# One core, state-space block and maxout FFN: full-array unread products, chunk 2's masks on GpSimd, a new order of the steps, weight-sum parts on VectorE

## Chip, cores and metric

One core of a Trainium2 chip. Times are device microseconds of one execution. The kernel before takes 240.26 us (median of 3 runs, 239.38 to 270.97). The profiled execution has its own time, 239.82 us, and a span of 238.1 us from its first to its last instruction.

## The reference, cut to what matters

Two blocks follow each other. The first is a chunked state-space scan for 4 batches, 8 heads, 768 positions, head dimension 32 and state size 16. Within a chunk:

```
cum = cumsum(log(clip(a)));  L = exp(cum_i - cum_j), causal
y  = ((C B^T) * L) x  +  (C state) * exp(cum)
state = exp(sum) * state + sum_j exp(cum_end - cum_j) B_j x_j
```

The result, 3072 tokens by 256 features, goes through a maxout FFN:

```
h   = max(max(y @ w1, y @ w2), y @ w3)      # w: 256 x 768
out = h @ w_out                             # 768 x 256
```

The weights come in as 64-bit floats and everything else as 32-bit.

## The kernel before

The sequence is cut into six chunks c = 0..5 of 128 positions, each of two halves g of 64. Feature groups of the FFN are f = 0..5, 128 wide; the weights are loaded and decoded in groups f0 = 0 (one f wide), 1 (one), 2 (two) and 4 (two).

What each engine does is a list of small named steps. The string ORDER at the top holds some 1,090 step names, and the program issues them in that order; `name/v` puts a step on another engine than its own (a ScalarE, v VectorE, p GpSimd, s SyncE's DMA queue, t TensorE). Every engine works its own steps strictly in this order, and a step waits for the tiles that it reads and for the buffer that it takes over. So the order is written out by hand in ORDER, and buffers of a kind (SLOTS; `ps` are the eight PSUM banks) are handed on in the order in which they come free.

Steps that the text speaks of:

- `ident`, `mask`, `ones`, `esel` and others (lines 200 to 282) make constants. `d.if0` loads group f0 of weight i (0, 1, 2 are w1, w2, w3; `o` is w_out), 64 bits as pairs of words, `ab cl sh lo pl sg` decode them to 32 bits (lines 640 to 675; `pl` on GpSimd), `df` subtracts w2 from w1 or w3 (`dd`), and `h.`/`l.` split a tile into a rounded high and a low part (`parts`, lines 677 to 684), since every product is made of three: high times high, high times low, low times high.
- `a.* clip ln scan pt0 pd1 pt1 left` make the running sum of log a for three spans of positions (0 to 128, 128 to 256, the rest), as bf16 parts in `left`. `right.c.p` copies rows of it by DMA on SyncE's queue. `mm.c.b` puts a mask into a PSUM bank by a product with a 128 x 128 identity (`mask_mm`, line 337), `em` (or `e` where no mask is there) adds the differences of the sums (`e_mm`), `xp` is the exponential on ScalarE into `L`. Where no mask product was made, `sel.c.p.g` sets the upper triangle to zero on GpSimd (`select`, line 365), four of them a chunk. Chunks 0, 1 and 2 use `mm`, chunks 3, 4 and 5 `sel`.
- `lB lC tB tC` load and transpose B and C of chunks 1 to 5 in 32 KB pieces; chunk 0 uses `lt`, `ltC` with turns on TensorE (`trB`, `trC`). `En E` are the decays from the chunk's start, `cd` or `ce` C times them, `bd` or `bk` B with its decay (`Bd`), `s` the scores C B (line 506), `w` the scores times `L` on VectorE, `A S so sa` the state, `yo` the product with the old state (line 518), `yw` the product within the chunk (line 530; `yw.c.g` for one half). `yH yL` split y.
- `up.c.f.i` (line 799) makes y @ (w1 - w2) or y @ (w3 - w2) for chunks 0, 1: six 512-column products, or a half with a fourth number; `m h hH hL` make the maximum and its parts.
- Chunks 2, 3 and 4, 5 go in pairs: seven products in place of eight per f (`q1` to `q7`, three matmuls each, line 818), for which differences `T.c.j` of the y parts and sums `ss` of the weight differences are made. `sw.f0.j` makes the four parts of `ss`, `h.ss`/`l.ss` split them. For groups 2 and 4 such a tile is 128 x 1024. `x1 e2 g7 c1 c2 mx hb ha hR hM` combine the seven.
- w2 itself, which the differences leave out of the maximum, is folded into w_out (`bt`, `b`, `fold`, `fo`), and `dn.c.term.z` (line 892) adds six h terms and two y terms, three parts each, into the output banks; `ob` copies them out, `st` stores them.
- `warm.n` (line 963) is a 512-column product of `ones`, whose result nobody reads. Eight stand at the very end of ORDER.

Of the kernel before, what the change touches and what calls it, by code (L numbers as in the profile page):

```python
# [29 lines left out]
xp.1.3 E.1 xp.1.2 lB.1.3 sh.02 left.2 s.0 mm.1.1 em.1.0 En.3 w.0.0 lx.0 En.2 mm.2.2 xp.1.1  # L30
w.0.3 xp.1.0 w.0.1 d.04 df.22 E.2 A.0 mm.2.1 w.0.2 yw.0.0 S.0.0 lB.1.5 E.3 lB.1.7 lB.1.0 ab.04
yH.0.0.0 pl.02 sg.02 df.02/v cl.04 sh.04 mm.2.3 yH.0.1.0 lB.1.6 h.up22 lB.1.2 lo.04 l.up22
pl.04 lB.1.1 tB.1 yo.0 yw.0.1 yH.0.1.1 yH.0.0.1 yL.0.0.0 h.up02 d.14 lo.14 tk.1 right.2.1
right.2.2 lC.1.3 yL.0.1.0 yL.0.1.1 ab.14 yL.0.0.1 En.5 right.2.0 em.2.1 S.0.1 d.24 ab.24 E.5
up.0.2.1 lC.1.7 lC.1.0 l.up02/v lC.1.5 up.0.3.0 so.0.1/v xp.2.2 xp.2.3 cl.14 sg.04 lC.1.4
sh.14 bk.1 m.0.3 lC.1.2 lC.1.1 lC.1.6 tC.1 lx.1 up.0.2.0 pl.14 sg.14 cd.1 df.04/v cm.1.1 cl.24
up.0.3.1 h.0.3 cm.1.0 s.1 m.0.2 h.0.2 sa.0.1 h.up04 l.up04/v w.1.3 mm.2.0 d.10 A.1 d.20 em.2.0
lo.24 right.3.0 up.0.5.0 xp.2.0 S.1.0 d.00 so.1.0 sh.24 lB.2.1 lB.2.4 w.1.1 sa.1.0 pl.24
xp.2.1 w.1.2 yo.1 w.1.0 ab.00 cl.00 lo.20 d.11 lC.2.4 lB.3.6 m.0.5 bt.2 ab.11 lC.3.4 sg.24
yw.1 cl.11 lC.3.7 df.24/v lo.10 ab.20 cl.20 lo.00/v lo.11/v h.up24 l.up24/v ab.10 cl.10  # L40
yH.1.1.0 lC.3.1 lB.4.4 h.b4 d.o2 sh.00 ab.o2 sh.10 sh.20 pl.10 yH.1.1.1 pl.00 right.3.1
yH.1.0.1 l.b4 hH.0.2 lB.2.2 up.0.4.0 up.0.5.1 S.1.1 yH.1.0.0 pl.20 lC.2.0 d.21 right.3.2
lB.2.3 up.0.4.1 yL.1.1.1 m.0.4 yL.1.1.0 yL.1.0.0 d.01 e.3.1 yL.1.0.1 xp.3.3 lo.01 sg.20 ab.01
sg.00 sg.10 up.1.4.0 df.00 h.0.5 up.1.2.0 sw.2.2 lC.2.1 lC.2.3 cl.01 sh.11 h.up00/v lC.4.1
lB.2.5 lB.3.5 up.1.4.1 lB.3.1 lC.3.5 pl.11 hH.0.3 df.20/v right.4.0 sh.01 lB.2.6 m.1.2 ab.21
sg.11 bt.1 h.up20/v bt.0 l.up20 lB.2.7 lo.21 lC.2.5 up.1.5.1 h.b2 m.1.4/v xp.3.2 h.1.4 pl.01
sg.01 d.o4 cl.21 lo.o2 l.up00/v h.b0 sw.4.2 sh.21 cl.o2 l.b0 lB.2.0 ab.o4 df.01 sh.o2 lC.4.3
lC.3.2 hH.0.5 e.3.0 xp.3.0 sw.2.0 cl.o4 lC.2.2 h.up01/v lC.2.6 lC.2.7 tC.2 cm.2.0/v up.1.0.1
up.1.5.0 lo.o4 pl.21 up.1.2.1 lx.3 m.1.5 l.up01 up.1.0.0 xp.3.1 up.0.0.1.0 sg.21 tB.2 lx.2
df.21 h.1.5 lB.4.1 h.0.4 sel.3.0.0 pl.o2 up.0.0.1.1 lC.3.0 tk.2 h.up21 up.0.0.0.0 cm.2.1 l.b2  # L50
h.1.2 m.1.0 bk.2 hH.1.2 h.1.0 s.2 sh.o4 d.o0 up.0.0.0.1 so.1.1/v right.5.2 w.2.1 A.2 pl.o4
w.2.3 m.0.0 lC.3.3 sw.1.0 cd.2 hH.1.5 lo.o0 S.2.0 sa.1.1/v so.2.0/v S.2.1 up.1.1.0 m.1.1/v
w.2.2 sel.3.0.1 up.1.3.0 up.1.3.1 hH.0.4 l.up21 w.2.0 m.1.3 h.0.0 lC.3.6 up.0.1.1 sa.2.0 yo.2
sg.o4 h.wo4 up.1.1.1 h.1.3 hL.0.3/v up.0.1.0 lB.3.3 yw.2 so.2.1/v l.wo4/v sg.o2 ab.o0 cl.o0
sh.o0 pl.o0 tC.3 cm.3.1/v m.0.1 h.wo2 cm.3.0 lt.3 lC.4.5 dn.0.h5.1 h.0.1 sa.2.1/v yH.2.0.0/v
dn.0.h3.2 right.5.1 yS.2.1.0/v lC.4.2 hL.0.4/v yH.2.1.1/v fold.4 dn.0.h4.2 hH.0.1 l.wo2/v
yS.2.0.1 sg.o0 right.4.1 yS.2.1.1/v right.4.2 yS.2.0.0 yH.2.1.0 dn.0.h4.1 lB.3.7 lB.3.0
yL.2.1.0 h.wo0 yL.2.0.0 l.wo0/v lB.3.2 yL.2.1.1 dn.0.h3.0 lB.3.4 tB.3 yH.2.0.1 yL.2.0.1 fold.2
fold.0 right.5.0 sel.3.1.0 sel.3.1.1 dn.0.h5.0 dn.0.h3.1 s.3 bd.3/v hH.0.0/v h.fo l.fo hL.0.5
# [58 lines left out]
def kernel(  # L118
# [48 lines left out]
    def fixed(name, shape, dtype=FP32):  # L167
        specs[name] = ("const", shape, dtype)
# [22 lines left out]
    def side(g):  # L191
        return slice(g * Q, (g + 1) * Q)
# [831 lines left out]
```

## Time and profile before

| | |
|---|---|
| median of the runs | 240.26 us |
| profiled execution, its own time | 239.82 us |
| its span | 238.1 us |
| mean granted TensorE clock | 0.95 |
| ScalarE busy | 94.7 us |
| GpSimd busy | 74.6 us |
| DMA: bytes moved, mean | 17.48 MB, 73 GB/s |

How to read what the prediction shows. PE is TensorE (PEld its weight loads), DVE VectorE, ACT ScalarE, POOL GpSimd, SPq SyncE's DMA queue. A row of a group gives the line, engine and operation, the tile written and the tiles read (buffer and group numbers are left out where they would part the group), the shape, the count, then busy time in us and the mean ns of one, and the idle time ahead of them with what ended it. A row of the timeline gives start and duration in us. Durations of consecutive instructions of an engine overlap a little at their ends. A row of the chain of waits gives start, length and who worked in that piece. A matmul's shown duration is longer than the distance to the next one, since matmuls are pipelined; the distance is what a stream of them costs.

### The profile page before, as it was taken

To read this page: it belongs to the slowest core of one execution; us is meant where nothing else is said; L and a number is where in the kernel's file an instruction comes from. 1 tells how busy PE (TensorE), PEld (TensorE's weight loads), DVE (VectorE), ACT (ScalarE), POOL (GpSimd) and SP (SyncE) were. 2 spreads that over 40 slices of the span, in tenths; PEclk is the share of its full clock that TensorE was granted. 3 is DMA by queue.
4 is the path that set the end of the run, shared out by engine and by line. 5 is a ranking of instruction groups with operands and counts; after the bars stand their busy time and mean duration, and the time that the engine had idled before them with its cause. 6 is when DMAs were issued, how large, how long until landed. Compare 5 with 4: busy or idle time off the path is not lost.

```text
span 238.1 us, 7045 instructions
## 1 busy us (share of the span) xinstructions
PE 221.8 (93%) x3004; PEld 185.9 (78%) x3004; DVE 202.4 (85%) x368; ACT 94.7 (40%) x183; POOL 74.6 (31%) x75
## 2 busy tenths in 40 slices
PE   4259999999999999999899999999999999999995
PEld 1135777877888897888688787999999888888993
DVE  5999689999999999699989899989887587999311
ACT  5496476867642520645340245141042314312001
POOL 3243432344651634002696580205300100042000
PEclk9755579999999999999999999999999999999999
DMA  5949697546940510122905009100000050000023
GB/s 146 186 105 191 165 171 211 158 103 160 155 117 3 67 24 3 26 57 58 151 3 66 0 5 139 50 6 4 3 3 0 0 176 3 0 0 0 3 89 133
DMA packets 65131, 17.48 MB, mean 73 GB/s; under 512 B 57804, under 2 KB 62668, under 8 KB 65100
## 3 DMA queue, kind: packets, MB, share of 16 engines
q1 hardware_dynamic: 64956, 16.78, 36.7%
q8 instruction: 23, 0.38, 0.7%
q10 hardware_dynamic: 144, 0.26, 0.5%
q14 instruction: 8, 0.07, 0.1%
HBM read 13.76 MB, written 3.15 MB: 71 GB/s over the span
## 4 chain that ended last, share of the span: by engine, by line
PE 57%; DVE 28%; SPq 4%; issue 4%; DMA 3%; ACT 2%; DVEq 0%
PE o L892 21%; PE E L818 8%; PE G L818 6%; PE u L799 6%; PE y L530 3%; SPq L402 3%; PE F L818 2%; PE H L818 2%; DVE L L189 2%; PE y L518 2%; DVE hL L189 2%; DMA raw<-in_moe_w_dram 2%; DVE Bd L189 2%; DVE h L922 2%; PE s L506 1%
## 5 line engine op out<-in xcount | busy, mean ns | idle before, releaser
L189 POOL TENSOR_TENSOR hL<-x,hH 128x512 fp32r<-128x512 f32 x8 | 11.0, 1390 | 46.0 <-DVE hH L186 25.8
L189 POOL TENSOR_TENSOR u<-u,r 128x512 uint32<-128x512 uint32 (+1 forms) x12 | 12.5, 1053 | 19.3 <-DVE u L660 15.5
L385 ACT ACTIVATE L<-e 128x512 f32<-128x512 f32 x24 | 13.5, 606 | 12.3 <-PE e L358 12.2
L189 DVE TENSOR_TENSOR L<-s,L 128x512 f32<-128x512 f32 x24 | 15.5, 678 | 0.0
L365 POOL TENSOR_SCALAR_AFFINE_SELECT L<-L 64x1024 f32<-64x1024 f32 x12 | 14.7, 1225 | 0.4
L184 ACT COPY g<-G 128x512 f32<-128x512 f32 x9 | 5.3, 589 | 21.2 <-PE G L818 13.8
L184 ACT COPY ob<-o 128x512 f32<-128x512 f32 (+1 forms) x11 | 5.9, 552 | 17.9 <-PE o L892 17.9
L189 POOL TENSOR_TENSOR hL<-h,hH 128x512 fp32r<-128x512 f32 x7 | 9.4, 1350 | 9.1 <-PE fold L768 5.2
L189 DVE TENSOR_TENSOR yL<-y,yH 128x256 fp32r<-128x256 f32 x24 | 9.5, 417 | 3.0 <-ACT yH L184 2.6
L184 ACT CAST hH<-x 128x512 fp32r<-128x512 f32 x8 | 4.9, 623 | 16.9 <-DVE x L860 12.4
L530 PE MATMUL y<-L,x 64*32 64x64 f32 x768 | 11.4, 240 | 0.0
L530 PEld LDWEIGHTS y<-L,x 64*32 64x32 f32 x768 | 10.1, 115 | 1.6 <-issue 0.6
L186 DVE COPY ob<-o 128x256 f32<-128x256 f32 (+1 forms) x3 | 1.5, 514 | 11.1 <-PE o L892 11.1
L189 DVE TENSOR_TENSOR e<-G,e 128x512 f32<-128x512 f32 x12 | 8.2, 686 | 2.3 <-PE G L818 2.1
L860 DVE SCALAR_TENSOR_TENSOR x<-e,x 128x512 f32<-128x512 f32 x12 | 9.9, 841 | 0.1
L877 DVE SCALAR_TENSOR_TENSOR hL<-g,hH 128x512 fp32r<-128x512 f32 x12 | 9.8, 832 | 0.1
L189 DVE TENSOR_TENSOR x<-F,x 128x512 f32<-128x512 f32 x12 | 8.2, 684 | 1.5 <-PE F L818 1.4
L189 DVE TENSOR_TENSOR g<-H,g 128x512 f32<-128x512 f32 x12 | 8.2, 682 | 1.4 <-PE H L818 0.7
L184 ACT CAST yH<-y 128x256 fp32r<-128x256 f32 x17 | 6.0, 376 | 8.6 <-PE y L530 6.8
L184 ACT COPY m<-u 128x512 f32<-128x512 f32 x10 | 5.8, 585 | 8.1 <-PE u L799 8.1
L892 PE MATMUL o<-wo4L,hH 128*128 128x256 f32 x48 | 8.4, 286 | 0.5 <-DVE ob L186 0.5
L189 DVE TENSOR_TENSOR g<-E,g 128x512 f32<-128x512 f32 x12 | 8.1, 684 | 0.8 <-PE E L818 0.6
(415 smaller groups left out, 707.4 us busy)
## 6 DMA issues: line engine op xcount, KB each, us to landing
raw<-in_moe_w_dram SPq DMA_DIRECT2D x6, 512.0 KB
x<-in_x_dram SPq DMA_DIRECT2D x6, 512.0 KB
out_dram<-ob SPq DMA_DIRECT2D x10, 256.0 KB
raw<-in_moe_w_dram SPq DMA_DIRECT2D x6, 256.0 KB
raw_o<-in_moe_w_out_dram SPq DMA_DIRECT2D x3, 512.0 KB
rawB<-in_B_dram SPq DMA_DIRECT2D x40, 32.0 KB
rawC<-in_C_dram SPq DMA_DIRECT2D x40, 32.0 KB
Bt<-in_B_dram SPq DMA_DIRECT2D x4, 256.0 KB
```

The lines of the kernel that those rows point to most:

```text
L184: nc.scalar.copy(out=to, in_=src)
L189: engines[e].tensor_tensor(out=to, in0=p, in1=q, op=op)
L365: nc.gpsimd.affine_select(out=part, in_=part, pattern=[[0, 2 * NH], [1, Q]], compare_op=ALU.is_ge, fill=0.0, base=0, channel_multiplier=-1)
L385: lambda e, c=c, b=b: nc.scalar.activation(at("L.%d" % c)[:, b], at("e.%d.%d" % (c, b)), AF.Exp))
L402: lambda e, raw=raw, src=src, r=r, hh=hh, tok=tok: engines[e].dma_start(out=at(raw)[rows(r), hh].rearrange("t b j n -> t b (j n)"), in_=sr ...
L518: nc.tensor.matmul(out=at("y.%d.%d.%d" % (c, r // 2, g))[q:q + 2 * D, b], lhsT=at("S.%d.%d" % (c, g))[rows(r), b].rearrange("p g d -> p (g ...
L530: nc.tensor.matmul(out=at("y.%d.%d.%d" % (c, t, g))[q * D:(q + 1) * D, b], lhsT=at("x.%d" % c)[side(g), b * NH + h], rhs=at("L.%d" % c)[si ...
L799: nc.tensor.matmul(out=o, lhsT=w[:, k, cols], rhs=v, start=(z == 0 and k == 0), stop=(z == 2 and k == KD - 1), skip_group_check=True)
L818: nc.tensor.matmul(out=at(bank), lhsT=w("HLH"[z]), rhs=y("HHL"[z]), start=(first and z == 0), stop=(z == 2), skip_group_check=True)
L860: nc.vector.scalar_tensor_tensor(out=at("x1." + cf), in0=at("e2." + cf), scalar=0.0, in1=at("x1." + cf), op0=ALU.max, op1=ALU.max))
L877: nc.vector.scalar_tensor_tensor(out=at("hL." + df), in0=at("g7." + cf), scalar=0.0, in1=plain(at("hH." + df)), op0=ALU.max, op1=ALU.subtr ...
L892: nc.tensor.matmul(out=at("o.%d.%d" % (c, b // 2))[:, b % 2], lhsT=left[:, b * P:(b + 1) * P], rhs=right, start=(first and b % 2 == 0), st ...
```

## The change

The edits:

- `ones` grows from 128 x 64 to 128 x 128, and a `warm` product takes all of it: 128 rows by 128 columns of weights, 512 columns streamed. The one other reader of `ones` takes 64 columns as before.
- `parts` of the weight sums has VectorE as its own engine instead of GpSimd. In the old order `l.ss1`, `l.ss0`, `l.ss4` were put on VectorE by name, so the one that moves is `l.ss2`.
- ORDER is replaced as a whole. It has 1,118 steps. `mm.2.0` to `mm.2.3` and `em.2.*` are gone, `e.2.*` and `sel.2.*` stand in their place. 36 `warm` steps stand between the first TensorE steps, up to the first `up` step, and none at the end. Weights are loaded in the order w1 of group 1, w2, w3 and w1 of group 0, w1 and w2 of group 2, then the others; before it was w2, w3 and w1 of group 2 first. Some 100 steps stand on another engine than before, about as many one way as the other.

The diff, with the new order cut to its first lines and its end:

```
-table mask ident ident16 parity d.12 a.0 own esel sel4 ind mm.0.3 ones nind minus0 anew ab.12
-a.1/s rowsel cl.12 sh.12 clip.0 lo.12 pl.12 mm.0.0 d.22 ln.0 scan.0 mm.1.3 ltC.0 clip.1 a.2
-sg.12 lB.1.4 mm.0.2 pt0.0 ln.1 scan.1 pd1.0 ab.22 pt0.1 pt1.0 lo.22 pd1.1 mm.1.2 lt.0 mm.0.1
...
-dn.5.h5.0.1.1 dn.5.h5.2.1.1 dn.5.h5.1.1.1 dn.5.h5.0.0.1 dn.5.h5.2.0.1 st.5.0.0 warm.2 warm.7
-warm.3 warm.1 ob.5.1.1/v st.5.1.1 warm.5 warm.4 warm.0 warm.6 ob.5.0.1/a st.5.0.1
+ones warm.9 warm.12 warm.27 d.01 d.10 ident own ind nind mask table a.0 esel sel4 anew ident16
+mm.0.3 mm.1.0 lo.01 warm.6 rowsel parity ab.01/v cl.01 sh.01 a.1/s warm.5 lo.10 pl.01 mm.0.0
+warm.30 mm.0.2 ab.10 cl.10 mm.1.1 warm.28 clip.0 minus0 warm.21 sh.10 pl.10 warm.23 ln.0
+scan.0 sg.10 pt0.0 pd1.0 a.2/s warm.15 warm.11 clip.1 warm.10 ln.1 pt1.0 left.0 clip.2
+spread.0 minus1 spread.1 d.20 lo.20 scan.1 ab.20 ln.2 scan.2 warm.3 d.00 pt0.1 d.02 ab.00
+pt0.2 warm.7 warm.26 ab.02 cl.20 em.0.1 pd1.2 warm.8 warm.16 mm.0.1 em.0.0 cl.02 warm.1 pd1.1
+warm.19 lo.00 warm.32 warm.17 sh.20 ltC.0 lt.0 warm.2 pt1.1 cl.00 En.0 left.1 warm.29 d.12
+sh.00 right.1.1 xp.0.2 pt1.2 lB.1.7 pl.20 warm.24 E.0 xp.0.0 lo.02 trC.0 warm.20 cq.0.1 xp.0.1
+ce.0 warm.33 pl.00 warm.34 lC.1.1 warm.31 warm.18 cq.0.0 trB.0 mm.1.2 xp.0.3 sg.01 warm.22
+cpB.0 warm.14 warm.0 sg.00 sg.20 warm.35 left.2 En.2 df.00/v s.0 ab.12 sh.02 right.1.0 bd.0/v
+right.1.2 em.1.0 cl.12 df.20/v sh.12 w.0.0 lx.0 E.2 mm.1.3 pl.02 En.1 lo.12 pl.12 w.0.1 d.11
+h.up00 w.0.3 h.up20 En.3 w.0.2 warm.25 E.1 em.1.1 xp.1.2 sg.02 E.3 A.0 xp.1.1 sg.12 lB.1.6
+S.0.0 l.up00 lB.1.4 ab.11 yo.0 xp.1.0 lo.11 S.0.1 yw.0.1 df.02/v cl.11 xp.1.3 lB.1.2 d.14
...
+dn.5.h5.0.1.0 dn.4.h1.2 st.2.1 ob.5.0.1 st.5.0.1 dn.4.y0.2 ob.5.1.0 dn.4.h1.0 ob.5.0.0
+st.5.0.0 dn.4.h1.1 dn.4.h5.0 st.5.1.0 ob.5.1.1/v st.5.1.1 dn.4.h5.2 dn.4.h3.2 dn.4.h0.1 ob.4.1
+st.4.1 ob.4.0/a st.4.0
...
-    fixed("ones", [P, Q], BF16)
+    fixed("ones", [P, P], BF16)
...
-                    out=e[side(g)], lhsT=at("ones")[rows(b)],
+                    out=e[side(g)], lhsT=at("ones")[rows(b), 0:Q],
...
-        parts(sums, sums, [P, 4, cols], kind, "p")
+        parts(sums, sums, [P, 4, cols], kind, "v")
...
-            out=at("warm.%d" % n)[0:Q], lhsT=at("ones"),
-            rhs=at("ones").unsqueeze(1).to_broadcast([P, NH, Q]), start=True, stop=True,
+            out=at("warm.%d" % n), lhsT=at("ones"),
+            rhs=at("ones").unsqueeze(1).to_broadcast([P, NB, P]), start=True, stop=True,
```

More of the change, by code (lines that the diff above doesn't have):

```diff
@@ L30 @@
[L30 to L47, printed above, removed]
@@ new lines @@
+l.up20/v sh.11 yH.0.1.1 yH.0.0.1 right.2.2 so.0.1/v yL.0.1.1 right.2.0 yL.0.0.1 right.2.1
+pl.11 sg.11 ab.14 cl.14 sh.14 warm.13 h.up02 lB.1.3 lB.1.5 lB.1.0 bt.1 h.b2 lB.1.1 df.01/v
+l.up02 warm.4 e.2.1 e.2.0 yw.0.0 up.0.0.0.1 lo.14 pl.14 h.up01 l.b2 yH.0.0.0 yH.0.1.0/v d.04
+yL.0.0.0 xp.2.2 yL.0.1.0 lC.1.4 tB.1 ab.04 sa.0.1/v up.0.0.1.1 cl.04 l.up01/v xp.2.1 lC.1.2
+sh.04 lC.1.0 lC.1.6 lo.04 up.0.2.0 m.0.2 lC.1.5 lC.1.3 lC.1.7 tC.1 xp.2.0 cm.1.0 tk.1 bk.1
+up.0.0.1.0 up.0.3.0 pl.04 up.0.0.0.0 cm.1.1 sg.14 sg.04 s.1 lx.1 m.0.3 m.0.0 df.04/v h.up04
@@ new lines @@
+dn.1.y1.1 T.2.3/p h.T.2.3/v dn.1.h4.2 sw.1.1 st.0.1 lB.4.1 hL.1.1 sel.4.1.0 q3.2.2 hL.1.3
+dn.1.h5.0 g7.2.2 q7.2.0 mx.2.2 hb.2.2 q3.2.3 q7.2.3 q6.2.3 q5.2.0 lC.5.5 g7.2.3/v g7.2.0
+so.3.1/v sa.3.1 lB.5.6 dn.1.y0.1 dn.1.h4.1 lC.4.1 dn.1.h2.1 mx.2.3 lC.4.0 lx.4 dn.1.h1.2
+right.5.0 l.T.2.3 q4.2.3 hL.1.2/v tC.5 dn.1.h4.0 sw.1.3 hR.3.2 sel.4.0.0 q2.2.3 dn.1.h0.2
+q4.2.0 e2.2.3/v q5.2.3 h.ss1 lt.4 sel.4.1.1 c2.2.3 lB.4.7 hb.2.3 q4.2.2 hR.3.3 c2.2.2 c1.2.3
+q7.2.5 q3.2.0 mx.2.0 right.5.1 dn.1.h1.0 sel.4.0.1 lC.4.6 q3.2.5 g7.2.5/v c2.2.0 dn.1.h5.2
```

132 lines of the change are left out of this document (65 added, 67 removed).

## The prediction

> **What bounds the kernel now.** I read the page's engine shares first, then the windows, the chain of waits, and the timeline at the places that the chain names.
>
> ```profile
> span 238.1 us, 7045 instructions
> PE 221.8 (93%) x3004; PEld 185.9 (78%) x3004; DVE 202.4 (85%) x368; ACT 94.7 (40%) x183; POOL 74.6 (31%) x75
> ...
> PEclk9755579999999999999999999999999999999999
> ...
> PE 57%; DVE 28%; SPq 4%; issue 4%; DMA 3%; ACT 2%; DVEq 0%
> ```
>
> The profiled execution took 239.82 us: this span and 1.7 us around it. The median of the runs shown is 240.26; the sum below is made against 239.82. TensorE and VectorE are both nearly full, the chain that ended last runs on both, and the granted clock is low in the second to sixth slice of about 6 us. By stage (busy us of PE, PEld, DVE, ACT, POOL; then clock, DMA share, GB/s):
>
> ```profile
> 12.00:18.00 6.00, 3.55 (x53) 2.21 (x58) 5.76 (x8) 5.91 (x12) 2.60 (x2) 0.50 0.40 105
> 24.00:30.00 6.00, 6.00 (x165) 4.96 (x165) 3.89 (x8) 2.80 (x7) 2.51 (x2) 0.50 0.66 176
> 30.00:36.00 6.00, 6.00 (x28) 4.51 (x27) 5.49 (x12) 4.75 (x10) 2.46 (x3) 0.76 0.95 154
> 0.00:36.00 36.00, 25.52 (x376) 17.07 (x377) 29.53 (x65) 23.43 (x43) 12.68 (x20) 0.67 0.83 159
> 0.00:24.00 24.00, 13.52 (x186) 7.61 (x186) 20.15 (x46) 15.88 (x27) 7.71 (x15) 0.69 0.84 157
> 0.00:114.87 114.87, 102.48 (x1714) 81.08 (x1714) 105.28 (x217) 63.32 (x123) 41.95 (x48) 0.90 0.58 112
> 114.87:233.95 119.08, 117.31 (x1282) 104.04 (x1282) 96.72 (x152) 30.99 (x59) 32.65 (x27) 1.00 0.19 35
> ```
>
> Up to 24 us TensorE idles 10.5 us while VectorE prepares decays and weights. From 24 to 30 TensorE is busy all the time, at half clock, and VectorE idles 2.1. Later the chain changes sides:
>
> ```profile
> 31.59 6.30 PE u L799 x24
> ...
> 102.36 0.41 PE e L358 x4
> ...
> 109.18 0.60 DVE T_1L L189
> ...
> 112.09 2.78 DVE ss0L L189
> ...
> 119.48 0.47 PE o L892 x4
> ...
> 121.60 0.69 PE E L818 x3
> ...
> 217.26 15.33 PE o L892 x126
> ```
>
> My anchor is 112.09 to 114.87, where the low part of group 0's weight sums (ss0L) on VectorE releases TensorE. A new order changes what VectorE has ahead of that step and what TensorE has behind it. Behind it TensorE has 77 of the seven-product steps (0.69 each) and 107 down steps (0.47): 53.1 + 50.3, with my estimate of 10.3 for the small products of chunks 4 and 5 113.7 us, in 119.1; so 5.4 us are waits.
>
> **The clock.** The same products, slow and fast:
>
> ```profile
> 24.15 1.93 PE L530 MATMUL y<-L,x 64*32 64x64 f32 x64
> 26.55 1.13 PE L518 MATMUL y<-Cd,S 32*64 32x64 f32 x32
> 29.48 1.11 PE L453 MATMUL tk<-ident,BT 128*128 128x128 f32 x4
> 31.52 1.22 PE L799 MATMUL u<-yH,up22H 128*128 128x512 f32 x2
> ...
> 154.85 1.48 PE L530 MATMUL y<-L,x 64*32 64x64 f32 x128
> ```
>
> At full clock 128 intra-chunk products take 1.48; in the opening 64 took 1.93. From 24.15 to the first up product at 31.52 stand two such halves, the old-state half, a turn-back, decays and masks: 7.4 us, of which about 3.1 would be left (the two halves by these rows, the rest halved). TensorE alone would gain 4.3. But VectorE follows at once and can give only what it idles there, 2.1 us and, from 30 to 36, 0.5. The clock's gain lies between 0 and 4.3, and I enter it below as idle time of VectorE that is won back.
>
> Do unread products lift the clock? From 24 to 30 small tiles keep TensorE busy 6.00 of 6.00 at 0.50; the grant rises in the next window, in which 128x128 arrays with 512 columns begin. So full arrays lift it. The page "TensorE: Matmul & The Clock Gate" of the Trainium skill, Part 1, says that some 3.4 us of sustained busy time are enough. By that alone the stage would have been fast from about 28, TensorE would gain 2 us there instead of 4.3, and the sum would come out about 1 us later. The row of 24 to 30 disagrees, and I go by the row.
>
> **The unread products** themselves:
>
> ```profile
> L337 PE MATMUL e<-mask,ident 128*128 128x512 bf16 x12 | 6.2, 600 | 2.5 <-DVE ident L186 2.5
> L963 PE MATMUL warm<-ones 128*64 128x512 bf16 x8 | 1.9, 382 | 0.0
> L365 POOL TENSOR_SCALAR_AFFINE_SELECT L<-L 64x1024 f32<-64x1024 f32 x12 | 14.7, 1225 | 0.4
> ```
>
> One costs 1.9 / 8 = 0.24 at full clock (128 columns of weights stream no longer than 64, as the mask products show), twice that at half. The 36 of the opening are 8.6 us, 17 if all run slow; they lie beside the 10.5 us in which TensorE idles. Nine in a row stand ahead of chunk 0's decays, 2.2 us or 4.3, beside VectorE's scan and spread. Without the cover up to 6.5 us would come onto the path. I take nothing. The eight at the end stand behind the last output product; removing them gives nothing.
>
> **Masks of chunk 2.** Four mask products go, 4 x 0.24 = 1.0 us of TensorE. Four selects come, 4 x 1.23 = 4.9 us on GpSimd, which is 31% busy. Behind them in its queue waits the decoding of w3's group 2, and on VectorE chunk 2's B with decay. I take them as hidden there, but GpSimd and VectorE hinder each other:
>
> ```profile
> 111.61 2.71 POOL L189 TENSOR_TENSOR ss2L<-ss,ss2H 128x1024 fp32r<-128x1024 f32 x1 [15.87 <-ACT ss2H L184]
> 112.09 2.78 DVE L189 TENSOR_TENSOR ss0L<-ss,ss0H 128x512 fp32r<-128x512 f32 x1
> L189 DVE TENSOR_TENSOR ss1L<-ss,ss1H 128x512 fp32r<-128x512 f32 x1 | 0.7, 680 | 0.0
> L189 DVE TENSOR_TENSOR L<-s,L 128x512 f32<-128x512 f32 x24 | 15.5, 678 | 0.0
> L189 DVE TENSOR_TENSOR yL<-y,yH 128x256 fp32r<-128x256 f32 x24 | 9.5, 417 | 3.0 <-ACT yH L184 2.6 <-ACT yS L184 0.3
> L186 DVE CAST T_1H<-T 128x512 fp32r<-128x512 f32 x2 | 0.8, 423 | 0.1
> L189 DVE TENSOR_TENSOR dd<-w,w 128x256 f32<-128x256 f32 x1 | 1.0, 977 | 0.0
> L189 DVE TENSOR_TENSOR ss4L<-ss,ss4H 128x1024 fp32r<-128x1024 f32 x1 | 2.0, 2042 | 0.0
> ```
>
> ss0L should take 0.68, as ss1L does; it took 2.78, ending just after GpSimd's ss2L. For the new selects I enter +0.8, between 0 and 2.4 (half of their time). The Trainium skill, "SBUF — State Buffer", section "Who interferes with whom", has an exclusive lock between a VectorE step with two SBUF inputs and a GpSimd step that reads SBUF; the ss0L row agrees. This speaks against the selects: by it each could hold VectorE for its whole length, 4.9 us, and the sum would come out 4.1 later; that is a part of rival 2.
>
> **The weight sums.** ss2L moves from GpSimd to VectorE. The block of ss0L goes: -2.1 (0 if another GpSimd step falls there). Its own work is in the next part. In all, VectorE goes from 365 steps to 359, ScalarE from 184 to 191, GpSimd from 68 to 70; four differences of y go to GpSimd at half of ss2L's 2.71 each. ScalarE is 40% busy and hides what it gains.
>
> **The order on VectorE.** Ahead of ss0L VectorE had 212 steps and now has 206; 36 have gone behind it or to other engines, 30 have come. Priced by width from the rows above (two inputs or from PSUM, 128x512: 15.5 / 24 = 0.65; 128x256: 0.40; casts 0.37; decoding bits 0.2): the 36 are ten of 0.65, ten of 0.40, six casts, two C masks of 0.5 and eight small ones, 15.4 us. The 30 are two of 1024 (ss2L, ss4L, 1.3 each), six of 0.65, twelve of 0.40, five casts and five small ones: 15.0, and 19.4 if the two take 2.04 and five of the 256 wide 0.98, as those rows show it beside GpSimd. So between -0.4 and +4.0; I take 0, since those long rows are blocked ones.
>
> Of the 114.87 us before the anchor's end VectorE idled 114.87 - 105.28 = 9.6, of that 36 - 29.53 = 6.5 up to 36. The opening now does group 0's and 1's smaller weights first, builds the identity ahead of the mask, and gets TensorE's results faster; but chunk 0's states stand behind 16 more weight steps (0.2 to 0.9 each) and three fewer, some 4.2 us of queue. I expect the first up product at about 30.3 instead of 31.5, and 2.0 of the 6.5 won back (0.5 to 3.5); of the 3.1 from 36 on 0.5.
>
> ```profile
> 10.75 1.06 PE L433 MATMUL trC<-ident,Ct 128*128 128x128 f32 x4
> 17.27 2.33 PE L506 MATMUL s<-CT,BT 32*64 32x128 f32 x64
> 20.32 0.74 DVE L314 SCALAR_TENSOR_TENSOR left<-t,nq,d 128x512 bf16<-128x512 bf16 x1
> ```
>
> DMAs: the load of C for chunk 0 now stands on SP's queue behind five weight loads and the third load of a, instead of two weight loads: 768 KB more, at the 157 GB/s of the row up to 24 about 5 us. Its turn on TensorE thus moves from 10.75 to 14 or so. Chunk 0's scores, at 17.27 before, now stand behind an En product that needs the third span of the decays (21 us before, perhaps 19 now); that covers it. Without the cover, up to 1 us. The third load of a moves to SP and frees ScalarE's queue; nothing.
>
> **The order on TensorE.** Of useful steps, before's queue had 18 ahead of the anchor that the new one has behind it or lost, and nine stand there anew. Net behind it: three seven-product steps, two decay steps, one En (0.2, my estimate), less one down step: 3 x 0.69 + 2 x 0.41 + 0.2 - 0.47 = +2.6; the mask products are taken off in it. Of the 5.4 us of waits behind it I expect 2.0 to go, as VectorE then has the sums of groups 2 and 4 done (0 to 3.3). The tail ends with two copies of 512 on ScalarE instead of halves on two engines: +0.3, at most 0.8.
>
> **The sum:** 0 (VectorE's steps) - 2.1 (block) - 2.0 - 0.5 (idle) + 0.8 (selects) + 2.6 (TensorE behind) - 2.0 (later waits) + 0.3 (tail) = -2.9: 239.82 - 2.9 = **236.9 us**, own range 234.8 to 239.5.
>
> **Rivals.**
> 1. The lock and the opening pay in full: idle -3.5, selects 0, later waits -3.3: 239.82 - 6.5 = 233.3. For it: TensorE alone would win 4.3 in the opening. Against: VectorE is busy 20.15 of the first 24 us and its queue ahead of the states is longer.
> 2. Slower: VectorE comes late to ss0L because its longer steps meet GpSimd: +4.0 for the steps, +2.4 for the selects, idle only -0.5, block -2.1, TensorE +2.6, no later gain, tail +0.3: +6.7, 246.5. It decides from the point where the last of the sums that the first seven-product stage reads ends after about 117 us. For it: the 0.98 and 2.04 rows. Against: GpSimd's load doesn't grow.
> 3. The change doesn't do what it says: the clock falls back in the gaps between the bursts of unread products (TensorE's waits for C, B and the third span), so the opening stays slow: idle won back 0 and 2 us of unread products on the path: 236.9 + 4.0 = 240.9. For it: from 12 to 18 TensorE was busy 3.55 of 6 us at 0.50. Against: 36 products, against six mask products before. The page "TensorE: Matmul & The Clock Gate" of the Trainium skill, Part 1, has the half clock come back after an idle window of about 3.4 us, which would be this rival.
>
> **Chances.** Forecast 0.40, rival 1 0.32, rival 2 0.13, rival 3 0.15. A measurement of this kernel tells about 2% from no change. Under 235.5: rival 1 and 0.02 of the forecast's lower edge, 0.34. Over 245: rival 2, 0.13. Between: 0.53. The range takes in rivals 1 and 3 and part of 2: 231.5 to 244.
>
> **What would show it.** Right: granted clock 1.00 in nearly all of 6 to 36; the first up product near 30; ss0L at about 0.7; fewer idle us of VectorE up to 36 (4.5 instead of 6.5); 36 unread products without a wait behind them. Wrong: clock 0.50 after 12 us (rival 3); VectorE's idle time gone and yet the sums end after 117 (rival 2); TensorE waiting less than 2 us after the sums (rival 1).

## The result and the profile after

The changed kernel takes 248.16 us (median of 4 runs, 245.94 to 248.76), the kernel before 240.68 beside it: ratio 1.0305, 95% interval 1.0265 to 1.0345, which is 7.3 us slower. The forecast was 236.9 with a range of 231.5 to 244.0; rival 2 (slower, 246.5) lay nearest. Ratios here and below leave out runs more than 1.5% above the fastest of their kernel, so that a median can stand higher than its ratio says (e12, where two runs remain, and e15); the profiled executions of these two are among those left out.

The page of the changed kernel; its line numbers stand three higher than those of before:

```profile
span 246.8 us, 7091 instructions
PE 227.1 (92%) x3028; PEld 186.5 (76%) x3028; DVE 203.9 (83%) x362; ACT 98.0 (40%) x191; POOL 84.4 (34%) x77
...
PEclk9999589999967999999999999999999999999997
...
PE 64%; DVE 18%; DMA 5%; issue 4%; SPq 4%; ACT 3%; ACTq 0%; DVEq 0%
...
L368 POOL TENSOR_SCALAR_AFFINE_SELECT L<-L 64x1024 f32<-64x1024 f32 x16 | 21.2, 1337 | 11.7 <-ACT L L388 11.5
...
L966 PE MATMUL warm<-ones 128*128 128x512 bf16 x36 | 12.6, 458 | 2.2 <-POOL ones L281 1.1
```

The opening's low clock has gone from most slices, but two dips stand in the row, one at 25 and one at 70 us. The 36 unread products took 12.6 us, 0.43 each up to 8.4 us and 0.22 from there, but for the last two, which fell into the first dip. The windows, with the columns as in the prediction, the last two cut at the new end of ss0L (the last one reaches 1.6 us beyond TensorE's last product, which ends at 242.1):

```profile
24.00:30.00 6.00, 5.07 (x166) 4.39 (x166) 3.79 (x12) 4.08 (x11) 1.98 (x2) 0.63 0.53 152
0.00:36.00 36.00, 29.58 (x414) 16.95 (x415) 31.20 (x80) 24.28 (x49) 14.06 (x21) 0.91 0.70 153
0.00:24.00 24.00, 18.51 (x154) 7.93 (x154) 21.44 (x58) 15.53 (x30) 9.47 (x18) 1.00 0.77 156
0.00:117.11 117.11, 105.86 (x1724) 80.38 (x1724) 106.73 (x211) 60.89 (x121) 50.57 (x50) 0.94 0.49 101
117.11:243.70 126.59, 121.27 (x1308) 106.14 (x1304) 97.22 (x153) 37.12 (x70) 33.80 (x27) 1.00 0.21 40
```

Up to 24 us the clock row reads 1.00 (0.69 before), though the first change on record, at 8.5 us, is the rise to full speed. VectorE idles 36 - 31.20 = 4.8 us up to 36 (6.5 before, 4.5 forecast). From 36 us to the anchor it idles 117.11 - 106.73 - 4.8 = 5.6 (3.1 before). Rows of the timeline (start, us) for the first up product and the anchor:

```profile
26.84 1.93 PE L533 MATMUL y<-L,x 64*32 64x64 f32 x64
...
32.73 0.50 PE L802 MATMUL u<-yH,up00H 128*128 128x256 f32 x2
...
116.43 0.69 DVE L192 TENSOR_TENSOR ss0L<-ss,ss0H 128x512 fp32r<-128x512 f32 x1
```

ss0L is no longer blocked (0.69 instead of 2.78), and still ends 2.2 us later than before. The first up product comes at 32.7 (31.5 before).

To see where TensorE loses, I add to a moment the TensorE work that is then still undone: each useful step at the median of its kind at full speed (a seven-product step 0.69, an up product 1.40, a down step 0.47, and so on). It is the time at which TensorE would end without another wait; unread products count nothing.

| at us | before | changed | e3, new order alone | e1, masks back |
|---|---|---|---|---|
| 45 | 224.4 | 224.2 | 226.4 | 225.6 |
| 55 | 223.9 | 226.3 | 226.6 | 228.0 |
| 75 | 224.2 | 231.8 | 229.0 | 230.4 |
| 95 | 226.4 | 233.4 | 230.7 | 231.2 |
| 115 | 228.9 | 234.3 | 232.8 | 231.8 |
| 155 | 231.2 | 236.7 | 234.4 | 234.4 |
| 205 | 232.1 | 240.1 | 238.1 | 238.1 |
| 225 | 233.3 | 242.2 | 239.7 | 239.7 |

At 45 us the changed kernel is level. It loses 8 us from 45 to 75, gets 2 back up to 115, where the old order has its own waits, and loses 3.5 more from 155 on.

### The profile page after: what moved, and what is told of

The parts are those of the page before. It is cut to its first block, busy times and chain, and to the rows that moved or that the text cites. A ratio compares the mean times of both kernels' runs of the same rounds, so it can differ in the third digit from the quotient of the medians.

```text
span 246.8 us, 7091 instructions
## 1 busy us (share of the span) xinstructions
PE 227.1 (92%) x3028; PEld 186.5 (76%) x3028; DVE 203.9 (83%) x362; ACT 98.0 (40%) x191; POOL 84.4 (34%) x77
## 4 chain that ended last, share of the span: by engine, by line
PE 64%; DVE 18%; DMA 5%; issue 4%; SPq 4%; ACT 3%; ACTq 0%; DVEq 0%
PE o L895 25%; PE E L821 9%; PE u L802 8%; PE G L821 5%; SPq L405 2%; DVE g L192 2%; PE y L533 2%; PE H L821 2%; DMA x<-in_x_dram 2%; PE F L821 2%; PE s L509 2%; DVE ss L192 2%; PE y L521 2%; DVE h L925 2%; DVE hL L880 2%
## 5 line engine op out<-in xcount | busy, mean ns | idle before, releaser
L368 POOL TENSOR_SCALAR_AFFINE_SELECT L<-L 64x1024 f32<-64x1024 f32 x16 | 21.2, 1337 | 11.7 <-ACT L L388 11.5
L192 POOL TENSOR_TENSOR u<-u,r 128x256 uint32<-128x256 uint32 (+1 forms) x12 | 13.7, 1148 | 21.1 <-DVE u L663 12.6
L966 PE MATMUL warm<-ones 128*128 128x512 bf16 x36 | 12.6, 458 | 2.2 <-POOL ones L281 1.1
L187 ACT COPY ob<-o 128x512 f32<-128x512 f32 (+1 forms) x9 | 4.9, 564 | 21.3 <-PE o L895 21.3
L187 ACT CAST hH<-h 128x512 fp32r<-128x512 f32 x9 | 5.4, 630 | 16.2 <-DVE h L925 16.2
L187 ACT COPY yS<-y 128x256 f32<-128x256 f32 x11 | 4.1, 382 | 18.9 <-PE y L533 18.7
L192 POOL TENSOR_TENSOR S<-S,old 128x256 f32<-128x256 f32 x5 | 3.7, 748 | 22.4 <-DVE old L192 11.8
L189 DVE COPY ob<-o 128x256 f32<-128x256 f32 (+1 forms) x5 | 2.6, 531 | 8.2 <-PE o L895 7.7
L895 PE MATMUL o<-wo0H,hL 128*128 128x256 f32 x48 | 7.9, 286 | 1.5 <-DVE hL L880 1.5
L925 DVE SCALAR_TENSOR_TENSOR h<-u,m 128x512 f32<-128x512 f32 x12 | 7.8, 679 | 1.3 <-PE u L802 1.3
```

Of the source, the lines that this page charges most:

```text
L187: nc.scalar.copy(out=to, in_=src)
L192: engines[e].tensor_tensor(out=to, in0=p, in1=q, op=op)
L368: nc.gpsimd.affine_select(out=part, in_=part, pattern=[[0, 2 * NH], [1, Q]], compare_op=ALU.is_ge, fill=0.0, base=0, channel_multiplier=-1)
L895: nc.tensor.matmul(out=at("o.%d.%d" % (c, b // 2))[:, b % 2], lhsT=left[:, b * P:(b + 1) * P], rhs=right, start=(first and b % 2 == 0), st ...
L925: nc.vector.scalar_tensor_tensor(out=at("h." + cf), in0=at("u.%s.1" % cf), scalar=0.0, in1=at("m." + cf), op0=ALU.max, op1=ALU.max))
L966: step("warm.%d" % n, "t", "warm.%d ones" % n, lambda e, n=n: nc.tensor.matmul(out=at("warm.%d" % n), lhsT=at("ones"), rhs=at("ones").unsq ...
```

## The experiments

Each was timed in 5 rounds against the kernel before (medians of it 240.2 to 240.6). In us, the ratio is taken times 240.3.

| run | median | ratio [95%] | against before |
|---|---|---|---|
| changed kernel | 248.16 | 1.0305 [1.0265, 1.0345] | +7.3 |
| e1 masks back on TensorE | 244.26 | 1.0165 [1.0118, 1.0213] | +4.0 |
| e2 no unread products | 249.03 | 1.0371 [1.0343, 1.0399] | +8.9 |
| e3 new order alone | 246.53 | 1.0244 [1.0198, 1.0290] | +5.9 |
| e4 ss2L back on GpSimd | 248.37 | 1.0346 [1.0298, 1.0394] | +8.3 |
| e5 old order, unread products | 250.41 | 1.0417 [1.0392, 1.0441] | +10.0 |
| e6 old order, selects | 242.87 | 1.0113 [1.0091, 1.0134] | +2.7 |
| e7 new order, then old | 246.01 | 1.0220 [1.0184, 1.0256] | +5.3 |
| e8 old order, then new | 245.32 | 1.0208 [1.0170, 1.0245] | +5.0 |
| e9 four TensorE steps moved | 243.51 | 1.0129 [1.0093, 1.0164] | +3.1 |
| e10 old order, ss2L on VectorE | 238.16 | 0.9914 [0.9880, 0.9947] | -2.1 |
| e11 old order, unread, rotating | 246.84 | 1.0246 [1.0198, 1.0294] | +5.9 |
| e12 old order, 29 tiny products | 250.10 | 1.0219 [1.0170, 1.0268] | +5.3 |
| e13 old order, 128 tiny products | 240.41 | 1.0000 [0.9976, 1.0023] | 0.0 |
| e14 differences back on VectorE | 244.86 | 1.0146 [1.0098, 1.0194] | +3.5 |
| e15 new order to 45 us | 254.87 | 1.0544 [1.0497, 1.0592] | +13.1 |
| e16 e10, unread, no shift | 240.38 | 0.9994 [0.9966, 1.0022] | -0.1 |
| e17 e1, unread moved | 243.35 | 1.0132 [1.0090, 1.0173] | +3.2 |

### One part undone: e1 to e4

**e1**, the new ORDER without the four selects:

```
-l.up02 warm.4 e.2.1 e.2.0 yw.0.0 up.0.0.0.1
+l.up02 warm.4 mm.2.2 mm.2.3 em.2.1 mm.2.0 mm.2.1 em.2.0 yw.0.0 up.0.0.0.1
```

> The changed kernel with chunk 2's masks back on TensorE (four mask products of 0.24 us; the four GpSimd selects are gone). Theory S, the selects are the loss: the VectorE steps beside them (from 46 to 51 and from 65 to 70 us) take their 0.68 and 0.42 us again, the half clock after 70 does not come, and the time falls from 248.2 by 4 to 6 to 242 to 244. Theory O, the order is the loss: the selects only filled VectorE's stretch while it was behind anyway; the time stays at 247 to 249, with the same wait of TensorE for up22L near 66 us.

Measured: 1.0165, so the selects cost 1.4% or 3.4 us (3.9 by the medians) net of the 1.0 us that they save TensorE. Theory S gets its size; but 4.0 us stay, and the wait for up22L stays too, as theory O has it. The timeline of the changed kernel where the first three selects run (POOL, then DVE):

```profile
46.25 3.96 POOL L368 TENSOR_SCALAR_AFFINE_SELECT L<-L 64x1024 f32<-64x1024 f32 x3
...
46.34 1.59 DVE L673 SCALAR_TENSOR_TENSOR w<-raw,u 128x512 uint32<-128x512 uint32 x1
47.85 1.36 DVE L660 TENSOR_SCALAR u_o<-u_o 128x512 f32<-128x512 f32 x1
49.13 1.61 DVE L192 TENSOR_TENSOR dd<-w,w 128x512 f32<-128x512 f32 x1
```

and the same three steps of e1:

```profile
47.66 0.69 DVE L673 SCALAR_TENSOR_TENSOR w<-raw,u 128x512 uint32<-128x512 uint32 x1
48.27 0.42 DVE L660 TENSOR_SCALAR u_o<-u_o 128x512 f32<-128x512 f32 x1
48.60 0.69 DVE L192 TENSOR_TENSOR dd<-w,w 128x512 f32<-128x512 f32 x1
```

Three steps of 1.8 us in all take 4.56. Of the selects' 3.96 us VectorE loses 2.8, also in the step with a single input. The fourth does it again, where TensorE waits (POOL, DVE, PE of the changed kernel):

```profile
65.45 1.15 POOL L368 TENSOR_SCALAR_AFFINE_SELECT L<-L 64x1024 f32<-64x1024 f32 x1
66.68 1.31 POOL L192 TENSOR_TENSOR u_o<-u_o,r_o 128x512 uint32<-128x512 uint32 x1
67.95 1.60 POOL L368 TENSOR_SCALAR_AFFINE_SELECT L<-L 64x1024 f32<-64x1024 f32 x1
...
65.68 1.19 DVE L192 TENSOR_TENSOR ss<-dd,dd 128x256 f32<-128x256 f32 x1
66.79 1.75 DVE L192 TENSOR_TENSOR up22L<-dd,up22H 128x512 fp32r<-128x512 f32 x1
68.47 1.22 DVE L192 TENSOR_TENSOR ss<-dd,dd 128x128 f32<-128x128 f32 x1
...
68.60 0.73 PE L802 MATMUL u<-yH,up22L 128*128 128x512 f32 x2 [1.51 <-DVE up22L L192]
70.73 1.11 PE L456 MATMUL tk<-ident,BT 128*128 128x128 f32 x4 [0.94 <-DVE BT L410]
```

After these waits the clock falls (70.0 to 76.8 us; tk takes 1.11 instead of 0.60). I set every VectorE step against the usual length of its form: of the changed kernel 24.9 us are stretch, of e1 21.0, and all of it lies beside GpSimd work. The kernel before has some 20 us of it too, so stretch accounts for the selects and not for the 4.0 us that stay.

**e2**, the `warm` steps keep their banks and emit nothing.

> The changed kernel without its 36 unread products, all else as it is. Theory V, VectorE paces the opening: the granted clock falls to about 0.5 from 12 to 30 us, the first up product stays within 1 us of 32.7, and the time within 1.5 us of 248.2. Rival C, the unread products do their work and the loss is elsewhere: the first up product comes 2 to 4 us later and the time is 250 to 252.

Measured: +8.9 instead of +7.3, so the unread products gain 1.6 us in the new order (0.9 by the medians; the intervals overlap). Theory V is right, its sign on the clock row is wrong: the granted clock reads 1.00 all through the opening, beside products at half speed (shown at the end of this document).

**e3**, e2's and e1's edits together, and `l.ss2/p`: the order alone.

> The new order alone: no unread products, chunk 2's masks on TensorE, ss2L on GpSimd as before. Theory S, the selects are the loss: within 2 us of the kernel before, 239 to 242. Theory O, the order is the loss: 246 to 249.

Measured: +5.9. Theory O: most of the loss is the order. In the table it is 2.0 us behind at 45, 4.8 at 75, 3.9 at 115 and 6.4 at 225.

**e4**, `l.ss2/p` in the changed kernel.

> The changed kernel with ss2L back on GpSimd. By the prediction's term VectorE loses its 1.3 us of work and gets the block of 2.1 back where a VectorE step of two inputs falls beside it: 248.2 plus 0 to 1. Rival: in the new order the move itself was a loss, VectorE being the engine that is late to the sums (the last low part ends at 117.1 instead of 114.9), and the time falls by 1 to 2.

Measured: +1.0 over the changed kernel, intervals overlapping. On GpSimd ss2L now holds not ss0L but the low part of an h of chunk 1 (106.61, 2.82 us instead of 0.68), which TensorE needs later.

### One part alone in the old order: e5, e6, e10, e11

**e6**, the old ORDER with `mm.2` issuing nothing and `em.2` unmasked, the selects behind chunk 1's parts and chunk 2's turn-back.

> The kernel before with chunk 2's masks by four GpSimd selects at the same places of the work (behind chunk 1's parts, and behind chunk 2's turn-back), its four mask products gone. Theory S, a select costs about 1 us wherever VectorE's steps meet it: 243 to 245, by the 3.9 that the selects cost in the new order. Rival: the cost belongs to the new order, in which VectorE is late; in the old one TensorE gains its 1.0 us and the time is 239 to 241.

Measured: +2.7. The selects cost where VectorE isn't late, too: theory S, a little below its range.

**e10**, `l.ss2/v` in the old ORDER.

> The kernel before with ss2L on VectorE, nothing else. By the prediction's term the block of ss0L (2.1 us) goes and 1.3 us of work comes to VectorE at the step that TensorE waits for: 240.3 - 0.8 = 239.5. Rival: ss2L stands ahead of ss0L on VectorE, TensorE's wait for ss0L is as long as before, 240.3 or up to 0.5 more.

Measured: -2.1 (0.9914), faster than both kernels and more than the 0.8 expected. The timeline of e10 (DVE):

```profile
112.01 0.69 DVE L189 TENSOR_TENSOR ss0L<-ss,ss0H 128x512 fp32r<-128x512 f32 x1
...
114.62 1.22 DVE L189 TENSOR_TENSOR ss2L<-ss,ss2H 128x1024 fp32r<-128x1024 f32 x1
```

The block is gone, and ss2L's own 1.2 us come behind ss0L, where TensorE has other work.

**e5** and **e11**, unread products in the old ORDER, e5 all into one PSUM bank, e11 each into the next free one:

```
-lt.0 mm.0.1 left.0 En.0 E.0
+lt.0 mm.0.1 warm.40 ... warm.53 left.0 En.0 E.0
...
-mm.2.1 w.0.2 yw.0.0 ... mm.2.3
+mm.2.1 w.0.2 yw.0.0 ... mm.2.3 warm.65 warm.66
```

> The kernel before with 38 unread products of 128x128 by 512 put into its own order up to 32 us (16 ahead of the first decays, the rest where TensorE waits), nothing else changed. Theory V, VectorE paces the opening: products at full speed there, but the first up product within 1 us of 31.5 and the time 239 to 241. Rival C, the clock of the opening is worth what TensorE alone would gain there: the first up product 2 to 4 us earlier and the time 236 to 238.

> The kernel before with 29 unread products in its own order, each in the next free bank (in e5 they all wrote one bank and took 0.43 to 0.64 us each, and the first state came 5.6 us late). Theory V: at 0.22 us each they fit into the gaps; 239.5 to 241. Rival C: the opening speeds up, 237 to 239. If they are late again (first state after 25 us), 242 or more.

Measured: +10.0 and +5.9, which neither theory had. e5 pushed the opening back by its products' length (0.43 to 0.64 us each), and lost some 5 us more in the waits shown next. In e11 they fit: at 45, 65 and 85 us it stands at 224.4, 224.6 and 226.1 in the sense of the table, level with before, though many products up to 36 us ran faster. So TensorE's clock in the opening brought the old order nothing, as theory V has it; a gain of up to 1 us isn't excluded, since a wait of 1.1 us of the kind shown next lies in e11's opening, at 27 us. Then e11 loses in a place that neither theory had named. Chunk 3's own product in e11:

```profile
95.85 1.43 PE L530 MATMUL y<-L,x 64*32 64x64 f32 x123
99.49 0.31 PE L530 MATMUL y<-L,x 64*32 64x64 f32 x5 [2.20 <-issue]
```

in the kernel before:

```profile
95.09 1.48 PE L530 MATMUL y<-L,x 64*32 64x64 f32 x128
```

and e11's waits of TensorE by cause (us in total, times, longest):

```profile
PE y L530 <- issue: 6.5, 5, 2.2
```

"Issue" is a wait that the trace gives no releaser for. The kernel before has none ahead of TensorE's products. The last three of them, 2.2, 0.8 and 1.5 us, lie behind 85 us, where e11 loses its 6 us.

### The instruction stream: e12, e13

**e12** and **e13** put tiny products into the old ORDER's first gap, 29 and 128:

```
+    step("tiny", "t", "tiny ones", lambda e: [nc.tensor.matmul(
+        out=at("tiny")[0:32, 0:1], lhsT=at("ones")[:, 0:32], rhs=at("ones")[:, 0:1],
+        start=True, stop=True, skip_group_check=True) for _ in range(29)])
...
-lt.0 mm.0.1 left.0
+lt.0 mm.0.1 tiny left.0
```

> The kernel before with 29 tiny unread products (32 columns of weights, one column) in TensorE's first gap of 5 us, as many instructions as e11 adds. Theory I, TensorE waits for its instructions: the waits come back in the small products of chunks 1, 3, 4 and 5, and the time is 245 to 247 as in e11. Rival C, e11's loss came of the unread products' work (clock, power, weights): 239.5 to 241.

> The same with 128 tiny products: with their weight loads 256 instructions, as many as one load of 16 KB from the instruction queue holds at 64 bytes each, so that every later product stands at the same place of a load as before. Theory I: the waits are gone again, 239.5 to 241.5. If each added instruction costs something by itself, or the waits don't come from a place in a load: 245 or more.

Measured: +5.3 for 29, 0.0 for 128. The waits of e12:

```profile
PE y L530 <- issue: 6.7, 4, 2.8
```

and chunk 3's product in e13, whole again:

```profile
94.92 1.49 PE L530 MATMUL y<-L,x 64*32 64x64 f32 x128
```

Theory I is shown: products that do nothing cost 5 us when they are 58 instructions (with their weight loads) and nothing when they are 256. The page's row of the instruction queue (loads, MB, share) in e11:

```profile
q8 instruction: 24, 0.39, 0.7%
```

gives 0.39 MB / 24 = 16 KB a load, 256 instructions of 64 bytes. Such a product issues 256 instructions in 1.5 us, weight loads with it. In e11 a load landed at 98.04 and TensorE went on at 99.49; in the changed kernel 49.21 and 50.60; in e1 50.60 and 51.89. The changed kernel has one such wait (1.2 us, in chunk 1's own product), e1 one of 1.4, e2 one of 0.4, e3 none: it is a part of what 36 more products cost, not the loss of the order.

The Trainium skill, "Runtime: NRT & Kernel Launch", section "Instruction fetch mechanics", has the stream refilled in 16 KiB blocks of 256 instructions, its cost mostly hidden. The size agrees with this row and with e13; that it is hidden does not hold for products this small.

### The order: e7, e8, e9, e14, e15

**e7** and **e8** (steps up to a cut from one order, the rest from the other):

> The new order of the steps up to chunk 3's own products (yw.3, at 99 us of the changed profile), then the remaining steps in the order of the kernel before; no unread products, chunk 2's masks on TensorE, ss2L on GpSimd. By the remaining work at 105 us the new order is 3 us behind there. Theory: half of the order's 6.4 us is lost before yw.3: 243 to 244. Rival E, all of it is lost in the early waits and the later part only carries it on: 246 to 247. Rival L, all is lost later: 240 to 241.

> The counterpart: the steps that the new order has up to yw.3 in the order of the kernel before, then the rest in the new order; no unread products, masks on TensorE, ss2L on GpSimd. Theory (half is lost later, in waits near A.5, q1.4.3 and q2.4.0 of together 3 us): 243 to 244. Rival E: 240 to 241. Rival L: 246 to 247.

Measured: +5.3 and +5.0. The halves add up to more than the whole (5.9): the seams cost by themselves; at 105 us e7 stands at 233.7 in the sense of the table, e3 at 230.8. So the two times don't decide between the theory and its rivals: with a seam in each, rival E too could give both. Where the order loses is told better by e3 in the table: 4.3 us are lost by 95 us, ahead of the seam, and 2.1 more by 225. **e15** cuts earlier:

> The new order up to chunk 1's first state (S.1.0, 43 us), then the remaining steps in the order of the kernel before; no unread products, masks of chunk 2 on TensorE, ss2L on GpSimd. By the remaining TensorE work the new order is 2.0 us behind at 45 us. Theory E, that loss is carried to the end: 242 to 243. Rival: VectorE has done more by then and gives it back, 240 to 241; if the seam costs, 244 or more.

Measured: +13.1: the seam costs, and the run tells nothing on its question.

**e9**, e1 with up.1.1.0, En.5, q1.4.2 and dn.5.h1.2 moved:

```
-up.1.4.1 h.1.4 up.1.3.1 lx.2 tk.2
+up.1.4.1 h.1.4 up.1.1.0 up.1.3.1 lx.2 tk.2
...
-q2.4.0 hM.5.3 dn.5.h1.2 hM.5.2 dn.5.h4.0 c1.4.0 dn.5.h3.1
+q2.4.0 hM.5.3 hM.5.2 dn.5.h4.0 c1.4.0 dn.5.h3.1 dn.5.h1.2
```

> The changed kernel with chunk 2's masks on TensorE (as in e1, 244.3) and four TensorE steps moved to where their operands have come: up.1.1.0 ahead of up.1.3.1 (which waits 1.8 us for up22L), En.5 four steps later (0.9), q1.4.2 one step later (0.7), dn.5.h1.2 two steps later (1.7). Theory W, the order's loss is these waits of TensorE: 244.3 - 4 = 240 to 241. Rival V, VectorE paces the whole and the waits only show it: they come back elsewhere, 243 to 245.

Measured: 0.9 us less than e1, intervals overlapping, and in the range of rival V: removing these waits doesn't bring the order's loss back. Even the 0.9 may be another thing, since e9's profile has 0.3 us of issue wait and e1's 1.4. **e14** goes at the late ones from the other side. This is how one looks in the changed kernel (POOL, DVE, PE):

```profile
214.89 2.98 POOL L192 TENSOR_TENSOR hL<-x,hH 128x512 fp32r<-128x512 f32 x2 [23.77 <-PE E L821]
...
216.66 1.75 DVE L880 SCALAR_TENSOR_TENSOR hL<-g,hH 128x512 fp32r<-128x512 f32 x1
...
218.46 0.74 PE L895 MATMUL o<-wo0H,hL 128*128 128x256 f32 x4 [1.49 <-DVE hL L880]
```

> The kernel of e1 (new order, chunk 2's masks on TensorE, 244.3) with the differences of y and their low parts, seven steps that the new order has on GpSimd, back on VectorE as in the order before. Theory X, GpSimd's collisions with VectorE make the late waits: 1 to 2 us less, 242 to 243. Rival V, VectorE sets the pace there and gets 4.8 us of work: 245 to 247.

Measured: 0.5 us less to 0.6 more than e1, by ratio or median: nothing. Both theories miss; the blocks that these seven steps make cost as much as the steps do on VectorE: the stretch of e14, reckoned as for e1, is 4.6 us less than that of e1, for 4.8 us more of work.

### The unread products' price: e16, e17

> The kernel of e10 (order before, ss2L on VectorE, 238.2) with 26 unread products of 128x128 by 512 in the gaps of the opening and 102 tiny ones, 256 instructions in all, so that the instruction loads fall where they fell. Theory V, VectorE paces the opening and the clock there is worth nothing: 237.5 to 239. Rival C: what TensorE alone would gain, 234 to 236.

Measured: 1.9 us over e10, with 0.3 us of issue wait. An unread product of e16 takes the bank that Cd's factors leave and waits for it:

```profile
PE warm L963 <- DVE Cd L189: 2.2, 1, 2.2
```

This wait isn't the loss: e11 has the same one, and its first state comes at 23.2 us, 0.5 earlier than before. Behind it e16 has two groups of tiny products that e11 hasn't, and from 15.8 to 22.6 us its clock is at half (in e11 from 15.2 to 18.7). Its timeline (PE, then DVE):

```profile
15.47 1.33 PE L972 MATMUL tiny<-ones 128*32 128x1 bf16 x45
...
23.34 0.83 PE L972 MATMUL tiny<-ones 128*32 128x1 bf16 x27
...
25.86 0.42 DVE L189 TENSOR_TENSOR S<-A,parity 128x256 f32<-128x256 f32 x1 [2.15 <-PE A L491]
```

VectorE waits 2.15 us for TensorE, the first state comes at 25.9 instead of 23.7, and those 2.2 us are carried to the end. So TensorE late in the opening cost about one for one here, and TensorE early gained nothing in e11; the padding that was to keep the loads in place is itself part of the lateness, so e16 is no clean price of the unread products.

> The kernel of e1 (new order, masks of chunk 2 on TensorE, 244.3, in two runs at a mean clock of 0.99 and more 242.4) with eight of its 36 unread products moved from 12 to 18 us into TensorE's gaps from 23 to 26 us. Theory K, the half clock from 26 to 33 us costs 2 us or more where TensorE is late: the clock holds and nearly all runs come to 242 to 243. Rival: the slower runs have another reason, 244 to 245 with the clock held.

Measured: 0.8 us less than e1, intervals overlapping (issue wait 0.4 us, in e1 1.4). The clock was not held, its fall came earlier (18.7 to 25.5 us instead of 26.2 to 33.0); whether the fall costs e1 its 2 us stays open. Of the changed kernel the one run at a mean clock of 0.999 took 245.9, those at 0.967 and 0.968 took 248.6 and 248.8. The runs of the kernel before, between 0.94 and 1.00, show no such step, but there a mean of 1.00 can also belong to a run at half clock all through the opening: the profile of e10 reads 1.00, and its first change on record is the rise at 33.3 us.

## Why the prediction was wrong, step by step

From profile to profile the span grew by 8.7 us: the anchor's end moved by 2.2 instead of -3.8 (0 - 2.1 - 2.0 - 0.5 + 0.8); TensorE has 3.2 more behind it (5.4 at 115 us in the table, less 2.2); the tail has 0.6 more; and the rest, 2.7, are waits behind the anchor. By the experiments, one part at a time: the order +5.9 (e3), the selects +3.4 (e1), the unread products -1.6 (e2), ss2L on VectorE -1.0 (e4, its interval overlapping). That is +6.7 of the 7.3 measured.

- **Later waits, -2.0: the largest miss.** They grew by some 2.7. I expected sums finished early to free TensorE; those of group 4 were (ss4L at 109 instead of 132 us; ss1L at 138 instead of 109), but TensorE then waits for other VectorE steps: behind A.5, q1.4.3 and q2.4.0 it waits 0.8, 0.6 and 1.5 us. Moving such steps (e9, e14) didn't bring the loss back, so it isn't theirs alone.
- **VectorE from 36 us on, -0.5: failed**, its idle time there rose by 2.5. I had counted its steps ahead of the anchor and not in which sequence TensorE needs them: w3's group 2 (up22L), done at 28.5 us in the old order, is done at 68.5 in the new, and an up product waits for it. In the kernel before:

```profile
27.18 1.28 POOL L189 TENSOR_TENSOR up22L<-dd,up22H 128x512 fp32r<-128x512 f32 x1 [5.00 <-ACT up22H L184]
```

  Nor had I asked when VectorE waits for TensorE. Its longest waits from 36 us to the anchor (us in total, times, longest), three of the changed kernel, then the longest of the kernel before:

```profile
DVE S L192 <- PE A L494: 2.2, 2, 2.0
DVE h L925 <- PE u L802: 1.3, 1, 1.3
DVE Bd L192 <- PE tk L456: 0.8, 1, 0.8
...
DVE yH L186 <- ACT yS L184: 0.9, 1, 0.9
```

  In the changed kernel VectorE waits 4.3 us for TensorE there, in the kernel before not at all: the two engines now wait for each other in turn.
- **Selects, +0.8: mis-sized**, 3.4 here and 2.7 in the old order, above the bound of 2.4. With the 1.0 us of TensorE that they save the gross price is 3.7 to 4.4 for 4 x 1.34 us. The section that the prediction cites, "SBUF — State Buffer", "Who interferes with whom", of the Trainium skill, had 4.9 by its exclusive lock: the measurement is nearer to it than to half of their time, by which I had bounded them; the ss0L row (2.1 of 2.71 us) had the size.
- **Opening, -2.0: right on VectorE** (4.8 idle, 4.5 forecast) **and worth nothing**: weight steps stand ahead of chunk 0's states that no early product reads (w1 of group 1, decoded from 4 us on, is first read at 40.7), the first up product came at 32.7 instead of 30.3, and at 45 us TensorE is level with before. In e11, in the old order, VectorE idles 1.3 us less up to 36 us, and TensorE is level at 45 as well.
- **Block of ss0L, -2.1: right**; in e10, where nothing else was changed, ss0L ends 2.2 us earlier; in the new order the block falls on another step (e4).
- **VectorE's steps ahead of the anchor, 0: within its bounds** as far as the rows tell: busy 106.73 against 105.28, the selects' blocks in it. My list of 30 new steps adds up to 14.2 and not 15.0, with its five small ones at 0.2 as in the list of 36; the term would have been -1.2 at its lower end.
- **TensorE behind the anchor, +2.6: right** (3.2). **Tail, +0.3:** +0.6, within its bound: from the end of TensorE's last output product to the end of the span 4.6 us instead of 4.0.
- **36 unread products, 0:** by e2 they gain 0.9 (medians) to 1.6 us (ratios) in the new order, the intervals overlapping, with 1.2 us of issue wait against 0.4 in it. The clock did fall back once they thin out, at 25.6 us, as rival 3 had it for the whole opening.

Rival 2's mark, a last sum after about 117, was only just met, at 117.1, and its price of 6.7 us was near, by luck in part, since its terms differ: the selects cost, yes; for longer decoding steps the rows show no room. That the new order costs 5.9 us by itself is shown (e3). Why it does is not: that VectorE's pace carries it fits e9 and e14 but is argued, and which of its moves cost most isn't settled, since pieces of the two orders don't fit together (e7, e8, e15).

## What to carry to other kernels

Price a new GpSimd step by 0.7 of its length or more where VectorE is as full as here, also beside VectorE steps with one input. A count of steps ahead of an anchor says nothing about an order; ask for each early product which step it waits for last, and for each VectorE step which product. And before adding or removing instructions on an engine with long runs of tiny ones, look for waits called "issue": the change of position alone was worth 0 (e13) or 5.3 us (e12) here.

## What the runs showed of the hardware

TensorE waits for its instructions: 2.2 us in one run of 128 small products in e11, 2.8 in e12, depending on where a 16 KB load begins (e11 to e13).

The granted clock reads 1.00 until its first change is on record, also beside products at half speed. In e3, without unread products, the first change is the rise at 37.2 us; a window ahead of it and the products in it:

```profile
18.00:24.00 6.00, 4.93 (x85) 3.19 (x84) 5.70 (x12) 3.58 (x8) 4.50 (x3) 1.00 0.99 143
...
19.00 2.01 PE L509 MATMUL s<-CT,BT 32*64 32x128 f32 x64
```

The same step takes 1.21 in the changed kernel, whose clock had risen at 8.5 us, and 1.21 later on in e3. So up to the first change the length of a product tells the clock, the row doesn't.

With unread products the lift came 3.1 (e16) to 5.9 us (e11) after the first unbroken run of full arrays began, 4.8 in the changed kernel, and the falls in the opening lasted 3.4 (e11) or 6.8 us (e1, e4, e16, changed kernel). The Trainium skill, "TensorE: Matmul & The Clock Gate", Part 1, has a free-running window of about 3.4 us for this; the falls agree with it, and the lift of e16 came a little sooner than one window.
